# Attention with global tokens and a token/channel MLP: q, k and v of batch 1 loaded ahead of the first channel weights, and the order of two stages rewritten

## The chip, the cores and the metric

The kernel runs on one core of a Trainium2 chip. The metric is device time in microseconds (us). The core has five engines that run their own instruction lists in order and wait for each other by semaphores: TensorE (PE; its weight loads are listed as PEld), VectorE (DVE), ScalarE (ACT), GpSimd (POOL) and SyncE (SP, which here only issues DMAs). DMAs are issued by SP and by GpSimd and are carried out by 16 DMA engines.

## The reference

Eight batches of 576 tokens, eight heads of 64. Attention is banded (32 to either side) with eight global tokens that see all and are seen by all; its result x (576 x 512) goes through an MLP over the tokens (576 to 256 to 576) and one over the channels (512 to 1536 to 512), each added to its input.

```python
scores = scale * np.matmul(q, k.transpose(0, 1, 3, 2))
mask = (np.abs(pos[:, None] - pos[None, :]) <= 32) | is_global[:, None] | is_global[None, :]
attn = softmax(np.where(mask, scores, -1e9))
x = np.matmul(attn, v)                               # then heads side by side: 8 x 576 x 512
h = np.maximum(x.transpose(0, 2, 1) @ w_tok1, 0.0) @ w_tok2
u = x + h.transpose(0, 2, 1)
out = u + np.maximum(u @ w_ch1, 0.0) @ w_ch2
```

## The kernel before

The heads are taken in two groups of four (hg 0 and 1). Per batch the steps are:

- *Loads.* `load_qk(b)` issues on SP one DMA of k and five of q for each head group (float32); `load_v(b)` five DMAs of v in 256-byte rows, into one of two buffers. q and k in float32 have one buffer each. For batches 1 and 2, `load_qk` begins with a four-byte DMA (line 132) that reads a corner of the channel weights `wc1` or `wc2`: it waits until those have landed, and everything behind it on SP waits with it.
- *Casts and transposes.* `cast_k` (GpSimd, line 145), `cast_q` (ScalarE, line 141) and `vcast` (GpSimd, line 198) make 16-bit copies. `Xk` and `Xq` (VectorE, lines 217 and 225 to 229) transpose k and q of one head group.
- *Scores.* `S_step(b, hg, part)` makes banded scores in PSUM (line 255) and their exponentials on ScalarE (264 to 270); VectorE multiplies by the band (`S_mask`, 281), and GpSimd copies the global columns (`S_eg`, 284). `GK` makes the rows of the global queries (296, exponential 300, mask 303).
- *Output of attention.* `OG` (309, its result scaled into `rf` at 315) is the global rows' sum over v; `PV(b, tau)` (329 to 342) the product with v for each of five token tiles; its `norm` on VectorE (348, 349) divides and gives x.
- *Token MLP.* `M1` (362, relu on ScalarE 365), `M2` (378, sum into u on VectorE 383 and 386), `M3` (transposes of u on TensorE 396 and 406, copied to `uT` by VectorE 399 and 408). For batch 0 there are variants by tile, `M2t` (547, sum 550) and `M3t` (558, copy on ScalarE 559).
- *Channel MLP.* `M4(b, j)` for twelve j (416, relu on ScalarE 419) and `M5(b, tau, part)` (442, sum 446, store by SP 447). The last 64 tokens of two batches are done together, in the odd batch (`M4l`, 429, 433; 449, 451).

PSUM has three rings: `pss` (two buffers), `psv` (one) and `psm` (two, for M4, M5 and the fill matmuls).

The order is written out by hand. A prologue takes batch 0 through attention and token MLP, with fill matmuls on zeros (`fill`, line 102) between. Then comes one period per batch b: the twelve to fifteen M4 steps (list D4), then the M5 steps (list D5), into which `merge` mixes the attention and token MLP of later batches. `merge(sparse, dense)` walks two lists of (cost, function) and always takes the one whose middle lies earlier as a share of its list's total cost; `gap(c)` is an entry of cost c that does nothing. `weave(a, z)` spreads the entries of z evenly among those of a. `later` puts off masks and norms by some steps. In the prologue, SP issues v of batch 0, then (behind the wait for `wc1`) q, k and v of batch 1; GpSimd issues the token weights and all of `wc1` after three casts of v; the casts and transposes of batch 1 stand behind batch 0's token MLP; and `load_wc2` stands behind three casts of batch 1's v.

Of the kernel before, what the change touches and what calls it, by code (L numbers as in the profile page):

```python
# [17 lines left out]
P = 128  # L18
# [13 lines left out]
def kernel(  # L32
# [56 lines left out]
    def load_v(b):  # L89
        for c in range(NT):  # L90
            r0 = WIN if c == 0 else 0
            r1 = P - WIN if c == NT - 1 else P
            j0 = P * c - WIN + r0
            nc.sync.dma_start(
                out=n32v[b % 2][r0:r1, c], in_=v[b, :, j0 : j0 + (r1 - r0), :].rearrange("h p d -> p h d")
            )

    def fill(n):
        if n:
            ps = psm([P, 512], name="w")  # L100
            for _ in range(n):
                nc.tensor.matmul(ps, lhsT=zz[:, 0:P], rhs=zz, start=True, stop=True)  # L102
# [4 lines left out]
    def alloc_16(b):  # L107
        s = st[b]
        s["q16"] = stg.tile([P, 2, RK * D], F16, tag="q16", name=f"q16_{b}")
        s["k16"] = stg.tile([P, 2, RK * D], F16, tag="k16", name=f"k16_{b}")  # L110
# [16 lines left out]

    def load_qk(b):
        alloc_32(b)
        if b in (1, 2):  # L130
            src = wc1[0:1, 0, 512:514] if b == 1 else wc2[0:1, 4, 0:2]
            nc.sync.dma_start(out=st[b]["k32"].bitcast(F16)[0:1, 0, 0:2], in_=src)
        for hg in range(2):
            nc.sync.dma_start(
                out=st[b]["k32"][:, hg], in_=k[b, 4 * hg : 4 * hg + 4].rearrange("h (i r) d -> (h i) (r d)", i=32)
            )
            load_q(b, hg)

    def cast_q(b, hg, half):
        f = slice(half * 9 * D, half * 9 * D + 9 * D)  # L140
        nc.scalar.copy(out=st[b]["q16"][:, hg, f], in_=st[b]["q32"][:, hg, f])  # L141

    def cast_k(b, hg, half, eng=None):
        f = slice(half * 9 * D, half * 9 * D + 9 * D)
        (eng or nc.gpsimd).tensor_copy(out=st[b]["k16"][:, hg, f], in_=st[b]["k32"][:, hg, f])  # L145
# [84 lines left out]
            out=dst[:, 4, NG : NG + 64].rearrange("p (i r) -> p r i", r=2), in_=src[:, 16:18]  # L230
        )

    def load_wc1():
        for h0 in range(0, NJ, 4):
            nc.gpsimd.dma_start(
                out=wc1[:, :, P * h0 : P * h0 + 4 * P],
                in_=moe_w_ch1[:, P * h0 : P * h0 + 4 * P].rearrange("(c p) x -> p c x", p=P),
            )

    def load_wc2():  # L240
        for h0 in range(0, NJ, 4):
# [60 lines left out]
    def GK_mask(b):  # L302
        nc.vector.tensor_mul(out=lfs[b % 2][:, 0:LW], in0=lfs[b % 2][:, 0:LW], in1=mf)

    def OG(b, get):
        ps = get([P, 2, 512], name=f"og_{b}")
        for c in range(NT):
            for r in range(4):
                nc.tensor.matmul(  # L309
                    ps[32 * r : 32 * r + 32, 0, 0 : 2 * VW].rearrange("p (g x) -> p g x", g=2), lhsT=egs[b % 2][:, c, r],  # L310
                    rhs=vsh[b % 2][:, c, r::4, :], start=(c == 0), stop=(c == NT - 1),
                )
        rf = mb.tile([P, H, VW], F16, tag="rf", name=f"rf_{b}")
        for hg in range(2):
            nc.vector.tensor_tensor(  # L315
                out=rf[:, 4 * hg : 4 * hg + 4, :],
                in0=ps[:, 0, VW * hg : VW * hg + VW].unsqueeze(1).to_broadcast([P, 4, VW]),
                in1=dsel[:, 4 * hg : 4 * hg + 4].unsqueeze(2).to_broadcast([P, 4, VW]), op=ALU.mult,
            )
        st[b]["rf"] = rf  # L320
# [34 lines left out]
    def M1(b, get):  # L355
        s = st[b]
        x16 = x16s[b % 2]
        ps = get([P, 2, 512], name=f"a1p_{b}")
        for ch in range(NT):
            for tt in range(2):  # L360
                w = w1[:, ch, P * tt : P * tt + P] if ch < NT - 1 else w1l[:, b % 2, P * tt : P * tt + P]
                nc.tensor.matmul(ps[:, tt, :], lhsT=w, rhs=x16[:, ch, :], start=(ch == 0), stop=(ch == NT - 1))  # L362
        a1 = mb.tile([P, 2, DM], F16, tag="a1", bufs=1, name=f"a1_{b}")
        for tt in range(2):
            nc.scalar.activation(out=a1[:, tt], in_=ps[:, tt], func=AF.Relu)
        s["a1"] = a1
        s["u16"] = mb.tile([P, 4, DM], F16, tag="u16", name=f"u16_{b}")
        s["ul"] = st[b - 1]["ul"] if b % 2 else mb.tile([P, DM], F16, tag="ul", name=f"ul_{b}")
# [41 lines left out]
    def M4(b, j):  # L410
        s = st[b]
        if j == 0:
            s["b1"] = mb.tile([P, NJ, 512], F16, tag="b1", bufs=1, name=f"b1_{b}")
        ps = psm([P, 512], name=f"b1p_{b}_{j}")
        for cc in range(4):
            nc.tensor.matmul(  # L416
                ps, lhsT=wc1[:, cc, P * j : P * j + P], rhs=s["uT"][:, cc, :], start=(cc == 0), stop=(cc == 3)
            )
        nc.scalar.activation(out=s["b1"][:, j, :], in_=ps, func=AF.Relu)  # L419

    def M4l(b, jj):
        s = st[b]
# [36 lines left out]
    def run(fn):  # L459
        fn()  # L460
        for e in pending:
            e[0] -= 1
        for e in [e for e in pending if e[0] <= 0]:
            pending.remove(e)
            e[1]()
# [33 lines left out]
    def u_PV(b, tau, get):  # L499
        def f():  # L500
            norm = PV(b, tau, get)
            later(LAG_PV, norm)
        return f

    def phase_s(b):
        return [(0.5, u_S(b, hg, part)) for hg in range(2) for part in range(2)] + [(0.9, u_GK(b, psv))]

    def phase_og(b):
        return [(0.3, lambda: OG(b, psv))] + [(0.8, u_PV(b, t, psv if t % 2 else pss)) for t in range(NT)]

    def phase_m(b):
        u = [(0.9, lambda: M2(b, 0, psv)), (0.9, lambda: M2(b, 1, pss)), (0.5, lambda: M2(b, 2, pss))]
# [48 lines left out]
    def X_units(b):  # L561
        fs = [lambda: Xk(b, 0), lambda: Xq(b, 0), lambda: Xk(b, 1), lambda: Xq(b, 1)]
        return [(0.0, f) for f in fs]
# [106 lines left out]
    def eg_const(i):  # L670
        for g in range(2):
            nc.gpsimd.tensor_copy(out=egs[i][:, :, :, g, NG:16], in_=ohk.unsqueeze(2).to_broadcast([P, NT, 4, NG]))
# [4 lines left out]
    nc.gpsimd.dma_start(out=w1l[0:LAST, 0], in_=moe_w_tok1[S - LAST : S, :])  # L677
    vcast(0, (2,))
    nc.gpsimd.dma_start(out=w2[:, :, 0:S], in_=moe_w_tok2.rearrange("(c p) x -> p c x", p=P))
    load_wc1()  # L680
    fill(FILL[1])
    u_S(0, 0, 0)()
    fill(FILL[2])
# [10 lines left out]
    )  # L694
    nc.vector.tensor_scalar(out=mf[:, 4 * QS :], in0=it_f[:, 4 * P : S], scalar1=gpp, scalar2=hi8, op0=ALU.is_equal, op1=ALU.max)
    globals_k(0, nc.vector)
    nc.gpsimd.memset(n32v[1][0:WIN, 0], 0.0)
    nc.gpsimd.memset(n32v[1][P - WIN : P, NT - 1], 0.0)
    make_identity(nc, ident)
    nc.gpsimd.memset(x16s[0][LAST:P, NT - 1, :], 0.0)  # L700
    nc.gpsimd.memset(x16s[1][0:LAST, NT - 1, :], 0.0)
    eg_const(1)
    globals_(1, nc.gpsimd)
    globals_k(1)
    load_qk(1)
    load_v(1)
    u_S(0, 1, 1)()
    vcast(0, (3, 4), nc.scalar)
    fill(FILL[8])
# [1 line left out]
    fill(FILL[3])  # L711
    flush()
    GK_mask(0)
    for i, (_, f) in enumerate(phase_og(0)):
        run(f)
        fill(FILL[4] if i == 0 else FILL[5])
    flush()
    run(lambda: M1(0, pss))
    fill(FILL[6])
    for _, f in phase_m0():  # L720
        run(f)
# [6 lines left out]
    def gap(c):  # L728
        return [(c, lambda: None)]

    def G(b):
        return zero(lambda: globals_(b, nc.gpsimd), lambda: globals_k(b))
# [15 lines left out]
    def M1u(b):  # L748
        return [(2.2, lambda: M1(b, pss))]
# [7 lines left out]
                k += 1  # L757
        return o + z[k:]

    alloc_16(1)  # L760
    for hg in range(2):
        for half in range(2):
            cast_k(1, hg, half)
            cast_q(1, hg, half)
    nc.gpsimd.dma_start(out=w1l[LAST:P, 1], in_=moe_w_tok1[S - LAST : S, :])
    vcast(1, (0, 1, 2))
    load_wc2()
    vcast(1, (3, 4))
    load_qk(2)
    load_v(2)  # L770
    load_v(3)
    for _, f in X_units(1):
        f()

    for b in range(B):
        D4, D5 = dense(b)
        if b == 0:
            merge(gap(2.5) + phase_s(1), D4)
            merge(gap(2.0) + weave(phase_og(1) + M1u(1), C(2)) + weave(phase_m(1), G(2) + X_units(2)), D5)
            flush()  # L780
            gather(gq, q, 1)
            gather(gk, k, 1)
        elif b == 1:
            merge(VC(2) + phase_s(2) + gap(1.0) + weave(phase_og(2) + M1u(2), C(3)), D4)
            for _, f in G(3) + X_units(3):
                f()
            gather_t(gq, gqT, 1)
            gather_t(gk, gkT, 1)
            merge(VC(3) + weave(mix(phase_m(2), phase_s(3))[:-2], C(4)) + mix(phase_m(2), phase_s(3))[-2:], D5)
            flush()  # L790
        else:
            A, Bs = [], []
            if b + 1 < B:
                A += phase_og(b + 1) + M1u(b + 1)
                Bs += phase_m(b + 1)
            if b + 2 < B:
                A = G(b + 2) + weave(A, X_units(b + 2) + VC(b + 2))
                Bs = mix(Bs, phase_s(b + 2))
            if b + 3 < B:
                Bs = weave(Bs[:-2], C(b + 3)) + Bs[-2:]  # L800
            merge(A, D4)
            merge(Bs, D5)
            flush()
# [30 lines left out]
```

## Time and profile before

| | us |
|---|---|
| median of 3 runs (347.11 to 347.55) | 347.35 |
| the profiled execution | 348.57 |
| its span, first to last instruction | 346.8 |
| TensorE busy (92% of the span) | 319.5 |
| VectorE busy | 189.1 |
| ScalarE busy | 161.0 |
| GpSimd busy | 74.7 |
| mean granted TensorE clock, share of full | 0.973 |

The page gives each engine's busy time, and then rows of 40 digits: each digit is the busy share of a slice of 8.67 us in tenths, or the granted clock in tenths of full speed. A row of a timeline has the start, the length, the engine, the line of the kernel, the operation, out<-in, shapes and the count, and in brackets the idle time of that engine before it and what ended it. "PE b1p L416" is the matmul of line 416 that writes the tile b1p. A row of the waits view has who waited for whom, the total, how often, and the longest.

### The profile page before, as it was taken

What the parts mean: (1) busy time and instruction counts of PE and PEld (TensorE: products, weight loads), DVE (VectorE), ACT (ScalarE), POOL (GpSimd) and SP (SyncE); (2) the same over time, 40 slices, a digit from 0 to 9 for tenths busy, and PEclk for the clock granted to TensorE, in tenths of its full rate; (3) what the DMA queues carried; (4) which work ended last, traced back from release to release, by engine and by line L of the source; (5) the groups of instructions that cost most, each with busy time, mean ns of one, the idle gap of its engine ahead of it and who ended that gap; (6) DMA issues with size and microseconds to landing.
All of it is one profiled execution on the core that took longest, in us unless ns stands there. A gap on an engine that the chain in (4) does not pass through costs nothing.

```text
span 346.8 us, 7500 instructions
## 1 busy us (share of the span) xinstructions
PE 319.5 (92%) x3092; PEld 163.1 (47%) x3092; DVE 189.1 (55%) x355; ACT 161.0 (46%) x301; POOL 74.7 (22%) x154
## 2 busy tenths in 40 slices
PE   6599867998899999998899999999899999999994
PEld 2236323554356444544466445544456446444641
DVE  7695622648668468735680578546771484153021
ACT  5570448530866274428445373447453444503600
POOL 5791360154062014101420014002400000000000
PEclk9699969999899999999999999999999999999999
DMA  7998979999984969901892139101000111011012
GB/s 156 188 152 189 214 142 159 237 169 249 240 216 116 193 178 261 205 2 61 229 191 52 62 109 229 30 30 63 34 2 2 60 62 32 0 62 60 2 60 91
DMA packets 55706, 41.55 MB, mean 120 GB/s; under 512 B 40952, under 2 KB 46968, under 8 KB 55672
## 3 DMA queue, kind: packets, MB, share of 16 engines
q1 hardware_dynamic: 50104, 36.59, 44.2%
q0 software_dynamic: 5568, 4.49, 8.6%
q8 instruction: 24, 0.39, 0.5%
q14 instruction: 10, 0.08, 0.1%
HBM read 36.12 MB, written 9.44 MB: 131 GB/s over the span
## 4 chain that ended last, share of the span: by engine, by line
PE 70%; ACT 6%; DVE 5%; issue 2%; POOL 0%; POOLq 0%; DVEq 0%; ACTq 0%
PE op L442 23%; PE b1p L416 21%; PE hp L378 5%; PE a1p L362 4%; PE s L255 4%; DVE e_all L281 3%; PE b1lp L429 3%; PE pv L337 2%; PE pv L329 2%; ACT e_all L264 2%; PE pv L342 2%; PE pu L396 2%; ACT e_all L270 1%; ACT e_all L269 1%; PE og L309 1%
## 5 line engine op out<-in xcount | busy, mean ns | idle before, releaser
L416 PE MATMUL b1p<-uT,wc 128*128 128x512 f16 x384 | 95.1, 390 | 4.2 <-ACT b L419 4.2
L442 PE MATMUL op<-wc,b 128*128 128x512 f16 x384 | 94.6, 379 | 0.0
L419 ACT ACTIVATE b<-b1p 128x512 f16<-128x512 f32 x96 | 57.4, 601 | 66.6 <-PE b1p L416 66.3
L281 DVE TENSOR_TENSOR e_all<-e_all,bandm 128x1000 f16<-128x1000 f16 x64 | 39.5, 679 | 31.5 <-ACT e_all L270 31.4
L416 PEld LDWEIGHTS <-wc 128*128 128x128 f16 x384 | 34.8, 99 | 44.2 <-issue 11.0
L442 PEld LDWEIGHTS <-b 128*128 128x128 f16 x384 | 34.8, 98 | 38.7 <-issue 4.2
L264 ACT ACTIVATE e_all<-s 128x800 f16<-128x800 f32 x32 | 25.1, 838 | 41.2 <-PE s L255 40.9
L446 DVE TENSOR_TENSOR osb<-u,op 128x512 f32<-128x512 f16 x32 | 21.9, 686 | 34.1 <-PE op L442 30.2
L383 DVE TENSOR_TENSOR u<-x,hp 128x1024 f16<-128x1024 f16 x14 | 17.1, 1221 | 41.1 <-PE hp L378 41.0
L284 POOL COPY eg<-e_all 128x160 f16<-128x160 f16 x14 | 4.6, 328 | 155.8 <-DVE e_all L281 151.2
L255 PE MATMUL s<-qT,kT 32*128 32x200 f16 (+1 forms) x640 | 22.8, 249 | 9.4 <-DVE qT L203 4.3
L349 DVE TENSOR_TENSOR x<-pv,rr 128x512 f16<-128x512 f32 (+1 forms) x40 | 27.6, 691 | 1.4
L337 PE MATMUL pv<-vsh,e_all 128*128 128x66 f16 x320 | 27.6, 193 | 0.0
L145 POOL CAST k<-k 128x576 f16<-128x576 f32 x28 | 17.8, 666 | 44.6 <-DVE kT L217 25.0
L337 PEld LDWEIGHTS <-e_all 128*128 128x128 f16 x320 | 24.0, 97 | 5.0 <-issue 0.4
L255 PEld LDWEIGHTS <-kT 32*128 32x128 f16 x640 | 13.0, 97 | 25.9 <-issue 23.1
L198 POOL CAST vsh<-v 128x512 f16<-128x512 f32 x38 | 23.0, 640 | 4.7 <-DMA v<-in_v_dram 4.7
L141 ACT CAST q<-q 128x576 f16<-128x576 f32 x28 | 18.3, 682 | 11.4 <-DMA q<-in_q_dram 11.4
L342 PE MATMUL pv<-vsh,e_all 128*128 128x66 f16 x256 | 23.4, 193 | 0.0
L102 PE MATMUL w<-zz 128*128 128x512 f16 x66 | 21.1, 434 | 1.3 <-DVE p_i L154 1.3
L329 PE MATMUL pv<-rf,lf 128*128 128x264 f16 x80 | 21.7, 275 | 0.4 <-DVE rf L315 0.4
L217 DVE STREAM_TRANSPOSE kT<-k 128x576 int32<-128x576 int32 x16 | 19.9, 1245 | 0.8 <-DMA k<-in_k_dram 0.5
(133 smaller groups left out, 351.5 us busy)
## 6 DMA issues: line engine op xcount, KB each, us to landing
q<-in_q_dram SPq DMA_DIRECT2D x64, 128.0 KB
out_dram<-osb SPq DMA_DIRECT2D x32, 256.0 KB
k<-in_k_dram SPq DMA_DIRECT2D x14, 576.0 KB
v<-in_v_dram SPq DMA_DIRECT2D x24, 256.0 KB
v<-in_v_dram SPq DMA_DIRECT2D x16, 192.0 KB
wc<-in_moe_w_ch_dram POOLq DMA_DIRECT2D x6, 512.0 KB, 8.8
q<-in_q_dram SPq DMA_DIRECT2D x16, 64.0 KB
out_dram<-osb SPq DMA_DIRECT2D x8, 128.0 KB
```

The source lines that it names most:

```text
L198: (nc.scalar.copy if eng else nc.gpsimd.tensor_copy)(out=vsh[b % 2][:, c, :, 0:D], in_=n32v[b % 2][:, c])
L255: nc.tensor.matmul(tiles[r // 2][:, r % 2, off : off + n], lhsT=kT[rs, P * c : P * c + P, e], rhs=qf[rs, lo : lo + n, e], start=(e == 0), ...
L264: nc.scalar.activation(out=e2[:, :, 1:3, 64:EW], in_=ps[:, :, 0:400].rearrange("p h (c x) -> p h c x", c=2), func=AF.Exp, scale=scale)
L281: nc.vector.tensor_mul(out=eh, in0=eh, in1=bandm)
L329: nc.tensor.matmul(ps[:, hf, 0 : 4 * VW], lhsT=lfs[b % 2][:, QS * tau - sh : QS * tau - sh + P], rhs=s["rf"][:, 4 * hf : 4 * hf + 4, :], s ...
L337: nc.tensor.matmul(o, lhsT=e_all[:, h, tau, QS - sh : QS - sh + P], rhs=vs[:, tau, h, :], start=False, stop=last and tau == NT - 1,)
L342: nc.tensor.matmul(o, lhsT=e_all[:, h, tau + 1, 0:P], rhs=vs[:, tau + 1, h, :], start=False, stop=last)
L349: nc.vector.tensor_tensor(out=x16[r, tau, :].rearrange("p (f h x) -> p f h x", f=2, h=4), in0=pq[r, :, :, 0:D], in1=rr[r].unsqueeze(3).to_ ...
L416: nc.tensor.matmul(ps, lhsT=wc1[:, cc, P * j : P * j + P], rhs=s["uT"][:, cc, :], start=(cc == 0), stop=(cc == 3))
L419: nc.scalar.activation(out=s["b1"][:, j, :], in_=ps, func=AF.Relu)
L442: nc.tensor.matmul(ps, lhsT=w, rhs=wc2[:, j, :], start=(j == 0), stop=(j == NJ - 1))
L446: nc.vector.tensor_add(out=osb, in0=s["u16"][:, tau], in1=ps)
```

## The change

- `load_qk(1)` and `load_v(1)` move up on SP, right behind batch 0's v, and the wait of `load_qk(1)` for `wc1` goes.
- `load_wc1` is cut into its three DMAs. On GpSimd they move behind the identity, the memsets of x16 and the globals of batch 1; the second follows the k casts of head group 0, the third those of head group 1. The memsets of v's edges, `eg_const(1)` and the load of `w1l` follow them.
- The q casts of batch 1 (ScalarE) move to before `phase_og(0)` for head group 0 and to behind `M1(0)` for head group 1. The transposes of head group 0 move to behind `M1(0)`; those of head group 1 stay behind the token MLP, now after `load_qk(2)` and `load_v(2)`.
- In batch 0's M4, the relus of odd j go to VectorE.
- In period 0, the gap of 2.5 ahead of batch 1's scores goes; batch 2's casts, next loads and globals are all woven into batch 1's OG, PV and M1; of batch 2's transposes the first pair goes ahead of M2(1) and the second between the second M3(1) and the third. `load_v(3)` moves to the end of the period.
- OG takes a `pss` buffer in place of `psv`. From period 2 on, a gap of 1.7 stands ahead of `phase_og(b + 1)`.

```diff
     def load_qk(b):
         alloc_32(b)
-        if b in (1, 2):
-            src = wc1[0:1, 0, 512:514] if b == 1 else wc2[0:1, 4, 0:2]
-            nc.sync.dma_start(out=st[b]["k32"].bitcast(F16)[0:1, 0, 0:2], in_=src)
+        if b == 2:
+            nc.sync.dma_start(out=st[b]["k32"].bitcast(F16)[0:1, 0, 0:2], in_=wc2[0:1, 4, 0:2])
...
-    def load_wc1():
-        for h0 in range(0, NJ, 4):
-            nc.gpsimd.dma_start(
-                out=wc1[:, :, P * h0 : P * h0 + 4 * P],
-                in_=moe_w_ch1[:, P * h0 : P * h0 + 4 * P].rearrange("(c p) x -> p c x", p=P),
-            )
+    def load_wc1(i):
+        nc.gpsimd.dma_start(
+            out=wc1[:, :, 512 * i : 512 * i + 512],
+            in_=moe_w_ch1[:, 512 * i : 512 * i + 512].rearrange("(c p) x -> p c x", p=P),
+        )
...
-        nc.scalar.activation(out=s["b1"][:, j, :], in_=ps, func=AF.Relu)
+        if b == 0 and j % 2:
+            nc.vector.tensor_scalar_max(out=s["b1"][:, j, :], in0=ps, scalar1=0.0)
+        else:
+            nc.scalar.activation(out=s["b1"][:, j, :], in_=ps, func=AF.Relu)
...
-        return [(0.3, lambda: OG(b, psv))] + [(0.8, u_PV(b, t, psv if t % 2 else pss)) for t in range(NT)]
+        return [(0.3, lambda: OG(b, pss))] + [(0.8, u_PV(b, t, psv if t % 2 else pss)) for t in range(NT)]
...
     nc.gpsimd.dma_start(out=w2[:, :, 0:S], in_=moe_w_tok2.rearrange("(c p) x -> p c x", p=P))
-    load_wc1()
+    load_qk(1)
+    load_v(1)
...
     globals_k(0, nc.vector)
-    nc.gpsimd.memset(n32v[1][0:WIN, 0], 0.0)
-    nc.gpsimd.memset(n32v[1][P - WIN : P, NT - 1], 0.0)
     make_identity(nc, ident)
...
-    eg_const(1)
     globals_(1, nc.gpsimd)
     globals_k(1)
-    load_qk(1)
-    load_v(1)
+    alloc_16(1)
+    load_wc1(0)
+    cast_k(1, 0, 0)
+    cast_k(1, 0, 1)
+    load_wc1(1)
+    cast_k(1, 1, 0)
+    cast_k(1, 1, 1)
+    load_wc1(2)
+    nc.gpsimd.dma_start(out=w1l[LAST:P, 1], in_=moe_w_tok1[S - LAST : S, :])
+    nc.gpsimd.memset(n32v[1][0:WIN, 0], 0.0)
+    nc.gpsimd.memset(n32v[1][P - WIN : P, NT - 1], 0.0)
+    eg_const(1)
     u_S(0, 1, 1)()
...
     GK_mask(0)
+    for half in range(2):
+        cast_q(1, 0, half)
     for i, (_, f) in enumerate(phase_og(0)):
...
     run(lambda: M1(0, pss))
+    xs = X_units(1)
+    xs[0][1]()
+    xs[1][1]()
+    for half in range(2):
+        cast_q(1, 1, half)
     fill(FILL[6])
...
-    alloc_16(1)
-    for hg in range(2):
-        for half in range(2):
-            cast_k(1, hg, half)
-            cast_q(1, hg, half)
-    nc.gpsimd.dma_start(out=w1l[LAST:P, 1], in_=moe_w_tok1[S - LAST : S, :])
     vcast(1, (0, 1, 2))
     load_wc2()
     vcast(1, (3, 4))
     load_qk(2)
     load_v(2)
-    load_v(3)
-    for _, f in X_units(1):
-        f()
+    xs[2][1]()
+    xs[3][1]()
...
-            merge(gap(2.5) + phase_s(1), D4)
-            merge(gap(2.0) + weave(phase_og(1) + M1u(1), C(2)) + weave(phase_m(1), G(2) + X_units(2)), D5)
+            merge(phase_s(1), D4)
+            merge(gap(2.0) + weave(phase_og(1) + M1u(1), C(2) + G(2)) + X_units(2)[:2] + phase_m(1)[:5] + X_units(2)[2:] + phase_m(1)[5:], D5)
             flush()
             gather(gq, q, 1)
             gather(gk, k, 1)
+            load_v(3)
...
-                A += phase_og(b + 1) + M1u(b + 1)
+                A += gap(1.7) + phase_og(b + 1) + M1u(b + 1)
```

## The prediction

> **What bounds the kernel now.** I read the page first: the span, the forty slices, the chain that ended last.
>
> ```profile
> span 346.8 us, 7500 instructions
> PE   6599867998899999998899999999899999999994
> PEclk9699969999899999999999999999999999999999
> PE 70%; ACT 6%; DVE 5%; issue 2%; POOL 0%; POOLq 0%; DVEq 0%; ACTq 0%
> ```
>
> TensorE is the bound: nearly every slice from the sixth on is full, and its work makes up 70% of the chain. So a gain can only come from TensorE's idle time and from slices with a lowered clock: the fifth and sixth (about 43 us) and the tenth and eleventh (about 86 us). The view by windows measures both places (columns: busy us of TensorE, weight loads, VectorE, ScalarE, GpSimd, then granted clock, DMA share, GB/s).
>
> ```profile
> 40.20:46.40 6.20, 1.97 (x10) 0.86 (x9) 4.60 (x6) 3.03 (x6) 2.28 (x4) 0.89 1.07 171
> 46.40:52.00 5.60, 5.60 (x14) 1.92 (x14) 0.50 (x2) 1.92 (x4) 4.43 (x8) 0.51 0.69 127
> 52.00:64.20 12.20, 10.29 (x141) 4.42 (x139) 4.97 (x9) 11.10 (x24) 0.70 (x3) 1.00 0.93 183
> 83.60:86.10 2.50, 0.79 (x11) 0.32 (x10) 2.40 (x5) 0.00 (x0) 0.00 (x0) 0.98 1.18 311
> 86.10:89.40 3.30, 3.30 (x42) 1.47 (x41) 3.00 (x5) 2.11 (x3) 0.00 (x0) 0.50 1.04 269
> 89.40:98.60 9.20, 7.70 (x100) 3.06 (x92) 5.40 (x11) 8.43 (x21) 0.71 (x3) 1.00 0.96 238
> ```
>
> The first stretch is batch 0's first channel product (line 416), the fourth the start of batch 1's. Who is late in the first is in the timelines of TensorE, ScalarE and SP's queue:
>
> ```profile
> 40.19 1.89 PE L416 MATMUL b1p<-uT,wc 128*128 128x512 f16 x8
> 46.32 6.34 PE L416 MATMUL b1p<-uT,wc 128*128 128x512 f16 x16 [4.24 <-ACT b L419]
> 64.17 2.10 PE L442 MATMUL op<-wc,b 128*128 128x512 f16 x9
> ```
>
> ```profile
> 33.89 1.08 ACT L365 ACTIVATE a<-a1p 128x512 f16<-128x512 f32 x2 [8.92 <-PE a1p L362]
> 36.62 0.58 ACT L559 COPY uT<-pu 128x512 f16<-128x512 f16 x1 [1.65 <-PE pu L558]
> ...
> 44.41 1.36 ACT L141 CAST q<-q 128x576 f16<-128x576 f32 x2 [3.15 <-DMA q<-in_q_dram]
> 45.68 1.08 ACT L419 ACTIVATE b<-b1p 128x512 f16<-128x512 f32 x2
> ```
>
> ```profile
> 9.54 5.41 SPq L94 DMA_DIRECT2D v<-in_v_dram  x5
> 29.70 0.68 SPq L132 DMA_DIRECT2D k<-wc  x1
> 31.38 0.35 SPq L134 DMA_DIRECT2D k<-in_k_dram  x1
> ```
>
> The relu of line 419 stands behind two casts of batch 1's second q half, these behind a DMA, and that behind SP's wait for the channel weights until 29.70. TensorE idles 4.24 us, and then works 5.6 us at a clock of 0.51.
>
> **The change, part by part.** *A, batch 0's first channel product.* SP no longer waits for the weights, so the five-DMA v load of batch 0 (issued 9.54 to 14.95) is followed at once by q, k and v of batch 1: 31.38 - 14.95 = 16.4 us earlier. Nothing else on SP moves ahead of work of batch 0. On POOL the three weight loads move behind the identity, two memsets and the globals, and the second and third of them behind the k casts of one half each:
>
> ```profile
> 17.60 0.58 POOL L677 DMA_DIRECT2D w1l<-in_moe_w_tok_dram  x1
> 18.15 0.65 POOL L198 CAST vsh<-v 128x512 f16<-128x512 f32 x1
> 18.71 0.76 POOL L679 DMA_DIRECT2D w<-in_moe_w_tok_dram  x1
> 19.42 2.28 POOL L235 DMA_DIRECT2D wc<-in_moe_w_ch_dram  x3
> ...
> 26.87 0.33 POOL L211 COPY kg<-gkT 128x16 f16<-128x16 f16 x2
> 35.96 1.28 POOL L145 CAST k<-k 128x576 f16<-128x576 f32 x2 [8.77 <-DMA k<-in_k_dram]
> 41.91 1.28 POOL L145 CAST k<-k 128x576 f16<-128x576 f32 x2 [4.67 <-DMA k<-in_k_dram]
> 48.28 0.61 POOL L198 CAST vsh<-v 128x512 f16<-128x512 f32 x1 [0.69 <-DMA v<-in_v_dram]
> 48.83 2.26 POOL L242 DMA_DIRECT2D wc<-in_moe_w_ch_dram  x3
> ```
>
> Where four ScalarE casts and two transpose pairs now run decides the gain. The casts of the first q half come behind batch 0's last exponential and ahead of line 365; ScalarE idles 8.92 us there, so they cost nothing if q lands by 32. The second half's casts stand between line 365 and the copies of line 559: 34.97 to 36.33, in the 1.65 us hole, if q has landed by 35. Before, the last q half was there 44.41 - 31.38 = 13.0 us after the first issue. From 14.95, plus some 3 us in which batch 0's v is still arriving (its third cast is at 18.15), that is 31, the low bound. The high bound lets every GpSimd load issued meanwhile go first. The loads issued from 16.8 to 21.7 were so far landed at 29.70 that SP went on, some 13 us; without the third weight load that is about 10 us, and q comes at 41. I take the middle, 36, because the second weight load cannot start before the first k half has landed. Casts then end at 37.4 and the first copy is 0.8 us late: **a loss of 0.8**, between 0 and 5.7.
>
> The transposes of the first half fall into VectorE's hole between these two:
>
> ```profile
> 31.90 0.68 DVE L349 TENSOR_TENSOR x<-pv,rr 64x512 f16<-64x512 f32 x1
> 35.44 1.33 DVE L550 TENSOR_TENSOR u<-x,hp 128x512 f16<-128x512 f16 x2 [2.86 <-PE hp L547]
> 40.78 1.24 DVE L217 STREAM_TRANSPOSE kT<-k 128x576 int32<-128x576 int32 x1
> 41.88 1.01 DVE L225 STREAM_TRANSPOSE qT<-q 128x512 int32<-128x512 int32 x1
> 42.75 0.20 DVE L229 STREAM_TRANSPOSE qT<-q 128x64 int32<-128x64 int32 x1
> ```
>
> 2.4 us in 2.86: free. If the hole were gone they would cost 2.4.
>
> What TensorE then has to do until line 442 starts is the busy time of the first three windows less what the clock took: 1.97 + 5.60 + 10.29 - 5.6 x 0.49 = 15.1 us. The stage now lasts 64.17 - 40.19 = 24.0. The 1.9 us of idle in the third window are score products waiting for exponentials (ScalarE is busy 11.10 of 12.20). They shrink, since the score steps are spread from the stage's start and six of twelve relus leave ScalarE. A VectorE relu is not in the trace; the nearest row is a 0.69 us operation of the same shape out of PSUM, so six take 4.1 us on an engine that had 4.97 of 12.2 us of work. I take 0.6 us of idle (between 0 and 1.9). The stage becomes 15.7: **a gain of 8.3**.
>
> *B, batch 1's u and its transposes.* At 83.6 VectorE has batch 2's transposes between TensorE's needs:
>
> ```profile
> 78.13 0.69 DVE L446 TENSOR_TENSOR osb<-u,op 128x512 f32<-128x512 f16 x1 [3.37 <-issue]
> 82.48 1.26 DVE L217 STREAM_TRANSPOSE kT<-k 128x576 int32<-128x576 int32 x1
> 83.77 0.69 DVE L399 COPY uT<-pu 128x1024 f16<-128x1024 f16 x1
> 84.38 1.03 DVE L225 STREAM_TRANSPOSE qT<-q 128x512 int32<-128x512 int32 x1
> 85.38 0.65 DVE L399 COPY uT<-pu 128x1024 f16<-128x1024 f16 x1
> 86.09 0.85 PE L255 MATMUL s<-qT,kT 32*128 32x200 f16 x14 [0.36 <-DVE uT L399]
> ```
>
> The first pair moves ahead of the M2 sums, into the 3.37 us hole before 78.13, the second behind both uT copies. The copies then run at 82.5 and 83.2, and the scores start at about 84.0 in place of 86.09: 2.1 us. The half clock of 86.1 to 89.4 costs 3.3 x 0.5 = 1.65 more, but behind it ScalarE is busy 8.43 of 9.20 and would take most of it back. **A gain of 2.5**, between 2.1 and 3.7. The five DMAs of batch 3's v go behind batch 3's q and k and the first output stores on SP; their cast comes a whole period later, so I cost that at nothing.
>
> *C, OG later.* These waits can go:
>
> ```profile
> PE og L309 <- POOL eg L284: 2.4, 5, 0.9
> ```
>
> ```profile
> 134.98 0.27 PE L329 MATMUL pv<-rf,lf 128*128 128x264 f16 x1 [0.45 <-DVE rf L315]
> 170.30 0.47 PE L309 MATMUL og<-vsh,eg 128*32 128x132 f16 x20 [0.90 <-POOL eg L284]
> 98.69 0.47 PE L309 MATMUL og<-vsh,eg 128*32 128x132 f16 x20 [0.19 <-POOL eg L284]
> ```
>
> The one at 98.69 lies in a period without the new gap. With weight 1.7 of then 8.2, OG is written behind three M4 steps (2.6 us), more than the longest wait. 2.4 - 0.19 + 0.45 = 2.7, less 0.3 for a step that finds the output buffer not yet drained: **a gain of 2.4**, between -1 and 2.7.
>
> **Sum.** -0.8 + 8.3 + 2.5 + 2.4 = 12.4 us. The profiled run took 348.57 us (span 346.8), 1.2 above the median of 347.35; it becomes 336.2, and the median **335.0**.
>
> **Rivals.** *1. The second q half comes late.* GpSimd's casting loads share the 16 DMA engines with SP's queue; then the old stall stands again, ahead of line 559. Against it, both weight loads behind the first are held back by k casts; for it, the DMA share is already about 1 in these windows. At 41 the loss is 5.7 in place of 0.8, 340; with a half clock behind it 2.7 more, 342.7. The Trainium skill, "DMA: Bandwidth & Descriptors", Queues, rings and completion order, says that each engine changes between its queues packet by packet, which speaks for a shared rate and so for this rival; no run here shows the share yet. The skill's "TensorE: Matmul & The Clock Gate", HAM oscillation, warns of idle gaps above some 3.4 us; by it, a stall shorter than that would leave the clock alone. The trace disagrees: 0.50 from 86.1 on follows 1.71 us of idle in 2.5, and this measurement decides.
>
> *2. The second channel weights come late.* They are issued behind three casts of batch 1's v, today at 48.83, and SP passes its wait for their second part at 58.46:
>
> ```profile
> 58.46 0.65 SPq L132 DMA_DIRECT2D k<-wc  x1
> ```
>
> The first product with them now starts at 40.2 + 0.8 + 15.7 = 56.7. If they came no earlier than now (the third part at about 60), TensorE would wait some 3 us: 338. I expect the issue near 42, as v is sent 16.4 us earlier and shares the engines for 10.
>
> *3. OG later gives nothing*, since its sums and the x it feeds come late for M1: 337.4. Against it:
>
> ```profile
> 182.25 0.68 DVE L349 TENSOR_TENSOR x<-pv,rr 64x512 f16<-64x512 f32 x1
> ```
>
> M1 starts 2.5 us after this ends, and a fifth of that is what the closer spacing takes.
>
> *4. Slower.* SP's transfers get only what GpSimd's leave, so the second q half lands at 46, later than today's 44.41, though sent 16.4 us earlier. Casts end at 47.4, the copies of line 559 are 10.8 us late, and one half-clock stretch adds 2.7: a loss of 13.5 in place of 0.8, which turns the sum into a loss of 0.3: 347.7. Each further us of landing is a us slower, so 349.7 at 48. It decides from a landing at 45.7 on.
>
> *5. The loads do not move* (SP held by a buffer of batch 0): q's buffer is one, but batch 0's casts read it out before 14.95, so I see nothing that holds it. Then the old stall stays in another place: 347.
>
> **How the numbers follow.** Forecast 55% (own range 332 to 338), rival 1 18%, rival 2 10%, rival 3 10%, rival 4 5%, rival 5 2%. A range of 331.5 to 341.5 takes in the forecast with B and C at their ends, rivals 2 and 3 and most of rival 1. A measurement of this kernel can tell 0.2% (0.7 us) from no change. Faster: 0.93; the same 0.03 (rival 5 and the edge of 4); slower 0.04.
>
> **What would show it.** A right: batch 1's q casts on ScalarE end before 37.5, no wait of TensorE for line 419's result, a clock of 1.0 from 40 to 57, and line 442 starting at 56 to 58. Rival 1: the first copy of line 559 behind a q cast waiting for DMA. Rival 2: line 442 waiting for wc. B right: no transposes between the uT copies and no clock drop near the second M4 stage. C right: no TensorE wait for eg of line 284 after the first. The forecast fails if TensorE's busy time at full clock is not what I took, or if the stall returns in front of the copies.

## The result, and the profile after

The changed kernel takes 336.28 us (median; 335.81 to 337.78), the kernel before 347.23 in the same series: a ratio of 0.969, 95% interval 0.966 to 0.973. In a second series it took 337.15 against 347.17 (0.973, 0.970 to 0.976). The prediction was 335.0, within 331.5 to 341.5. The profiled execution took 337.78, with a span of 336.1.

The page of the changed kernel, the same rows as before:

```profile
span 336.1 us, 7493 instructions
PE   7499999988999999999999999999999999999994
PEclk9789999999999999999999999999999999999999
PE 78%; ACT 7%; DVE 6%; DMA 5%; issue 2%; POOL 1%; SPq 0%; ACTq 0%; DVEq 0%; POOLq 0%
```

Behind the first three slices the clock's row stays at 9, and no slice of TensorE's row is under 8 until the last. DMA is new in the chain, with 5%: the chain now runs through the load of batch 2's q, which makes TensorE wait (below).

Batch 0's first channel product is now line 414, its relus 420 (ScalarE) and 418 (VectorE), the second product 443. The timelines of TensorE, ScalarE and VectorE of the changed kernel around it:

```profile
41.18 1.03 PE L414 MATMUL b1p<-uT,wc 128*128 128x512 f16 x4
...
50.96 2.83 PE L414 MATMUL b1p<-uT,wc 128*128 128x512 f16 x12 [0.81 <-DVE b L418]
...
56.64 2.11 PE L443 MATMUL op<-wc,b 128*128 128x512 f16 x9
```

```profile
34.87 1.08 ACT L363 ACTIVATE a<-a1p 128x512 f16<-128x512 f32 x2 [6.24 <-PE a1p L360]
35.84 1.33 ACT L140 CAST q<-q 128x576 f16<-128x576 f32 x2
37.60 0.59 ACT L560 COPY uT<-pu 128x512 f16<-128x512 f16 x1 [0.42 <-PE pu L559]
```

```profile
33.49 1.24 DVE L216 STREAM_TRANSPOSE kT<-k 128x576 int32<-128x576 int32 x1
34.58 1.03 DVE L224 STREAM_TRANSPOSE qT<-q 128x512 int32<-128x512 int32 x1
35.46 0.21 DVE L228 STREAM_TRANSPOSE qT<-q 128x64 int32<-128x64 int32 x1
36.42 1.33 DVE L551 TENSOR_TENSOR u<-x,hp 128x512 f16<-128x512 f16 x2 [0.76 <-PE hp L548]
```

The stage lasts 56.64 - 41.18 = 15.5 us (before: 24.0). The second q casts need no wait for the DMA, and the first copy waits for TensorE, not for them. The first transposes lie where the 2.86 us hole was and leave 0.76 us of it. But the stage begins at 41.18, 1.0 later than before.

The end of batch 1's token MLP and the start of its M4, in the changed kernel's timelines of TensorE and ScalarE:

```profile
72.12 1.30 PE L376 MATMUL hp<-a,w 128*128 128x512 f16 x4 [1.56 <-ACT a L363]
78.36 0.66 PE L253 MATMUL s<-qT,kT 32*128 32x200 f16 x16
78.95 1.04 PE L414 MATMUL b1p<-uT,wc 128*128 128x512 f16 x4
```

```profile
70.10 1.48 ACT L140 CAST q<-q 128x576 f16<-128x576 f32 x2 [5.32 <-DMA q<-in_q_dram]
71.48 1.08 ACT L363 ACTIVATE a<-a1p 128x512 f16<-128x512 f32 x2
```

From the first score step on (78.36) the transposes are in nobody's way; ahead of it stands a wait that the kernel before did not have: M1(1)'s relu behind casts of batch 2 that wait for a DMA. In the later periods the waits for eg are gone, and two of 0.18 us for an output buffer are in their place:

```profile
PE og L307 <- POOL eg L282: 0.2, 1, 0.2
PE b1p L414 <- DVE osb L447: 0.4, 2, 0.2
PE b1p L414 <- ACT b L420: 0.7, 1, 0.7
```

The third row is one wait at the head of batch 2's M4. It was there in six of the nine runs below that have the gap ahead of OG, without a pattern that I could find; its cause stays open.

### The profile page after: what moved, and what is told of

Read it like the earlier page. It is cut to its first block, busy times and chain, and to the rows that moved or that the text cites. A ratio compares the mean times of both kernels' runs of the same rounds, so it can differ in the third digit from the quotient of the medians.

```text
span 336.1 us, 7493 instructions
## 1 busy us (share of the span) xinstructions
PE 316.1 (94%) x3092; PEld 162.2 (48%) x3092; DVE 193.9 (58%) x361; ACT 158.1 (47%) x295; POOL 75.5 (22%) x154
## 4 chain that ended last, share of the span: by engine, by line
PE 78%; ACT 7%; DVE 6%; DMA 5%; issue 2%; POOL 1%; SPq 0%; ACTq 0%; DVEq 0%; POOLq 0%
PE op L443 23%; PE b1p L414 22%; PE s L253 5%; PE hp L376 5%; PE a1p L360 4%; DMA q<-in_q_dram 4%; PE b1lp L430 3%; DVE e_all L279 3%; ACT e_all L262 3%; PE w L102 3%; PE pv L335 3%; PE pv L327 2%; PE pv L340 2%; PE gk L294 2%; PE pu L394 2%
## 5 line engine op out<-in xcount | busy, mean ns | idle before, releaser
L414 PE MATMUL b1p<-uT,wc 128*128 128x512 f16 x384 | 92.9, 379 | 1.9 <-DVE b L418 0.8
L420 ACT ACTIVATE b<-b1p 128x512 f16<-128x512 f32 x90 | 53.9, 599 | 62.6 <-PE b1p L414 62.3
L279 DVE TENSOR_TENSOR e_all<-e_all,bandm 128x1000 f16<-128x1000 f16 x64 | 42.0, 717 | 19.1 <-ACT e_all L268 19.0
L253 PE MATMUL s<-qT,kT 32*128 32x200 f16 (+1 forms) x640 | 22.0, 245 | 7.6 <-DVE qT L202 4.9
L144 POOL CAST k<-k 128x576 f16<-128x576 f32 x28 | 18.7, 698 | 39.5 <-DMA k<-in_k_dram 22.0
L197 POOL CAST vsh<-v 128x512 f16<-128x512 f32 x38 | 24.0, 667 | 11.6 <-DMA v<-in_v_dram 11.6
L102 PE MATMUL w<-zz 128*128 128x512 f16 x66 | 21.9, 448 | 1.3 <-DVE p_i L153 1.3
L376 PE MATMUL hp<-a,w 128*128 128x512 f16 x72 | 19.3, 378 | 2.7 <-ACT a L363 1.6
```

The costliest lines, as they stand in the source:

```text
L253: nc.tensor.matmul(tiles[r // 2][:, r % 2, off : off + n], lhsT=kT[rs, P * c : P * c + P, e], rhs=qf[rs, lo : lo + n, e], start=(e == 0), ...
L279: nc.vector.tensor_mul(out=eh, in0=eh, in1=bandm)
L376: nc.tensor.matmul(ps[:, i, :], lhsT=w2[:, ch, P * tau - sh : P * tau - sh + P], rhs=s["a1"][:, ch, :], start=(ch == 0), stop=(ch == 1),)
L414: nc.tensor.matmul(ps, lhsT=wc1[:, cc, P * j : P * j + P], rhs=s["uT"][:, cc, :], start=(cc == 0), stop=(cc == 3))
```

## The experiments

Theory: the change gains in three separate places, as predicted (A the first channel product, B the place of batch 2's transposes, C OG's start), and loses at two, one in the prologue and one at M2(1). The rivals are that the steps overlap, or that another part of the edit did it. The runs come in three series, each with the kernel before in it (medians 347.17, 347.56 and 347.16). The changed kernel itself ran in the first of them, with 337.15; from "The channel weights' three parts at once" on, the comparison with it goes across series.

### The changed kernel again, as the yardstick

> The changed kernel itself, as the yardstick for the three that run beside it. Expected 336.3 (335.8 to 337.8), 11 us below the kernel before. Its first score product started 0.55 us later in the profile of the change than in the profile of before (13.12 against 12.57), ahead of every edit. Theory: that is a difference between executions, so it moves by some tenths again here. Rival: the change itself makes it late, and it stands at 13.1 again.

Measured: 337.15. The first score product began at 12.54, so its 0.55 us in the first profile was a difference between executions. M1(0) still began at 32.38, 0.85 behind the 31.53 of before: this lateness belongs to the change.

### C undone: no gap ahead of OG

```diff
-                A += gap(1.7) + phase_og(b + 1) + M1u(b + 1)
+                A += phase_og(b + 1) + M1u(b + 1)
```

> The changed kernel without the gap of 1.7 ahead of OG; everything else stays. Theory (step C): the waits for eg come back, 0.9, 0.2, 0.9 and 0.2 us, and 0.4 for rf, while some 1.0 us of new waits at the head of M4 go: 1.6 slower than the changed kernel, 337.9. Rival (OG later gives nothing, the gain of the later periods came from something else, such as the output buffer of OG): within 0.4 of it.

Measured: 338.87, 1.7 slower than the changed kernel in the same series. The waits view of this kernel has the old row again, to the tenth:

```profile
PE og L307 <- POOL eg L282: 2.4, 5, 0.9
```

OG used the other PSUM ring here too, so that edit does not take these waits away; the gap does.

### All of batch 0's relus on ScalarE

```diff
-        if b == 0 and j % 2:
-            nc.vector.tensor_scalar_max(out=s["b1"][:, j, :], in0=ps, scalar1=0.0)
-        else:
-            nc.scalar.activation(out=s["b1"][:, j, :], in_=ps, func=AF.Relu)
+        nc.scalar.activation(out=s["b1"][:, j, :], in_=ps, func=AF.Relu)
```

> The changed kernel with all twelve relus of batch 0 on ScalarE. Theory (step A: the odd relus had to leave ScalarE, since it is the tight engine while scores and M4 run mixed): ScalarE gets six times 0.6 more in the 15.5 us of that stage, TensorE's idle time there grows from 1.0 to 2 to 3 us, so 1 to 2 slower, 337.3 to 338.3. Rival: the relu on VectorE is what makes TensorE wait (0.81 us at 50.96 for a relu behind the masks), ScalarE has room, and it is equal or up to 0.8 faster.

Measured: 336.26, 0.9 faster than the changed kernel beside it. The stage itself was 0.5 longer (41.37 to 57.24), and the later start met a shorter wait at M2(1) (0.32). So the theory's sign held for the stage, with a quarter to a half of its size, and not for the whole. Where the 0.9 comes from the traces do not show: the two profiled executions are 0.14 apart (336.64 and 336.78), and the changed kernel's own two series differ by as much as 0.9.

### Batch 2's second casts behind M1(1)

```diff
-            merge(gap(2.0) + weave(phase_og(1) + M1u(1), C(2) + G(2)) + X_units(2)[:2] + ...
+            merge(gap(2.0) + weave(phase_og(1), C(2)[:3]) + M1u(1) + C(2)[3:] + G(2) + X_units(2)[:2] + ...
```

> The changed kernel with the k and q casts of batch 2's second half (and the loads of batch 3 behind them) written behind M1(1), so that M1's relu does not stand behind casts that wait for a DMA. Theory: the 1.56 us wait of TensorE at 72.12 is ScalarE's order and goes, 1.3 to 1.6 faster, 334.8. Rival: it is the late DMA itself, which then holds up the second transposes of batch 2 and the later score steps instead: within 0.5 of the changed kernel.

Measured: 335.96, 1.2 faster than the changed kernel beside it. No wait at M2(1) is left, and no new one stands for it later. It was ScalarE's order: the q itself comes early enough for its own transposes. This wait also hides what happens ahead of it. In eight of the nine traces that keep the casts ahead of M1(1)'s relu, those of the changed kernel and of the edits below included, M2(1) begins 58.6 to 59.2 us behind the first score product, although M1(0) lies anywhere from 19.0 to 20.3 behind it; in the ninth (the last experiment) it is 59.9. With the casts behind the relu it is 57.1.

### The channel weights' three parts at once

```diff
     load_wc1(0)
+    load_wc1(1)
+    load_wc1(2)
     cast_k(1, 0, 0)
     cast_k(1, 0, 1)
-    load_wc1(1)
     cast_k(1, 1, 0)
     cast_k(1, 1, 1)
-    load_wc1(2)
```

> The changed kernel with all three parts of the first channel weights issued together, ahead of the k casts: the second part some 1 us and the third some 7 us earlier than in the change, and both inside the flight of batch 1's second q half. Theory (holding the parts back is what lets q land by 36): the second q half lands 2 to 4 us later, ScalarE's casts behind M1(0)'s relu wait for the DMA until 38 to 40, the copies of line 560 slip by 1.5 to 3.5, and the whole is 1.5 to 4 slower than the changed kernel (337.2 in its last series), 338.7 to 341. Rival: SP's queue keeps its rate beside GpSimd's loads, nothing slips, within 0.5.

Measured: 337.85 (ratio to before 0.972, 0.968 to 0.976), not told apart from the changed kernel's 337.15. ScalarE's timeline in it:

```profile
36.84 0.67 ACT L140 CAST q<-q 128x576 f16<-128x576 f32 x1
37.72 0.67 ACT L140 CAST q<-q 128x576 f16<-128x576 f32 x1 [0.21 <-DMA q<-in_q_dram]
38.60 0.59 ACT L560 COPY uT<-pu 128x512 f16<-128x512 f16 x1 [0.20 <-PE pu L559]
```

The cast waits 0.21 us and holds nothing up. But the place had become later too: the band masks took 4.36 us, M1(0) began 20.3 us behind the first score product (19.4 and 19.8 in the two profiles of the changed kernel), and the wait at M2(1) hid that. (One of the four masks took 1.13 us from 23.62 on, where it takes 0.67 undisturbed, though GpSimd's casts began only at 25.10; up to then it issued the three loads. What slowed that mask is open.) The second half of q landed at 37.72; in two kernels further down, which hold the parts back and whose cast waits for q as well, it landed at 36.90 and 36.26. That is 0.8 and 1.5 us earlier, of which half a us is SP's, which issued batch 1's k at 15.60 here (15.10 and 15.01). So holding the parts back does not bring the 5 us that lie between the prediction's 36 and its high bound; the reason it gives for taking the middle was too weak. The Trainium skill's "DMA: Bandwidth & Descriptors", Queues, rings and completion order (engines change between queues packet by packet), is not contradicted.

### B undone: batch 2's transposes in their old places

```diff
-            ... + X_units(2)[:2] + phase_m(1)[:5] + X_units(2)[2:] + phase_m(1)[5:], D5)
+            ... + phase_m(1)[:3] + X_units(2)[:1] + phase_m(1)[3:4] + X_units(2)[1:2] + phase_m(1)[4:5] + X_units(2)[2:3] + phase_m(1)[5:] + X_units(2)[3:], D5)
```

> The changed kernel with batch 2's transposes put back to where they stood before, between M2(1) and M3(1) and between the M3(1) steps. Theory (step B): the uT copies stand behind 2.4 us of transposes again, TensorE idles some 1.7 us before the second M4 stage and then meets a half clock for about 3.4 us: 2 to 3 slower than the changed kernel, 339.2 to 340.2. Rival: what bounds that stage is ScalarE's exponentials and the q casts, so the transposes' place is worth under 0.7.

Measured: 339.41 (0.978, 0.972 to 0.984), 2.3 above the changed kernel's 337.15 (1.9, if each is taken from the kernel before of its own series). TensorE's timeline has the three old waits again, 0.78, 0.57 and 0.35, and the next M4 starts 81.06 - 78.95 = 2.1 later than in the change. The window of the idle time:

```profile
79.02 0.38 PE L404 MATMUL pul<-ident,ul 128*128 128x128 f16 x4 [0.78 <-DVE uT L397]
79.98 0.26 PE L253 MATMUL s<-qT,kT 32*128 32x200 f16 x2 [0.57 <-DVE qT L228]
80.59 0.54 PE L253 MATMUL s<-qT,kT 32*128 32x200 f16 x14 [0.35 <-DVE uT L397]
81.06 1.04 PE L414 MATMUL b1p<-uT,wc 128*128 128x512 f16 x4
```

```profile
77.00:82.00 5.00, 3.29 (x38) 1.63 (x35) 4.97 (x7) 0.84 (x2) 0.00 (x0) 1.00 1.02 267
82.00:87.00 5.00, 3.64 (x51) 1.60 (x51) 4.00 (x8) 4.73 (x11) 0.00 (x0) 1.00 0.92 248
```

The same 1.7 us of idle, and yet a clock of 1.00: the half clock that followed in the kernel before is not a sure consequence of it.

### The kernel before, its stall filled with matmuls

The edit computes nothing new: 19 matmuls on zeros into a buffer that nobody reads.

```diff
+        if b == 0 and j == 2:
+            pf = pss([P, 2, 512], name="pf")
+            for _ in range(19):
+                nc.tensor.matmul(pf[:, 0], lhsT=zz[:, 0:P], rhs=zz, start=True, stop=True)
```

> The kernel before, with 19 matmuls on zeros (4.1 us of TensorE work into a spare buffer) written just ahead of batch 0's third M4 step, where TensorE idles 4.24 us. The stall itself stays. Theory (step A: the half clock from 46 to 52 is made by the idle time, and cost 2.7): the clock stays at 1.0 there and the stage is 2.0 to 2.7 shorter: 344.5 to 345.2. Rival: the clock falls all the same, or the exponentials behind it take the gain back: 346.5 to 347.2.

Measured: 346.06 against 347.56 (0.996, 0.994 to 0.998): 1.5 faster. TensorE's timeline and the window that had a clock of 0.51:

```profile
42.46 4.26 PE L417 MATMUL pf<-zz 128*128 128x512 f16 x19
46.56 3.62 PE L420 MATMUL b1p<-uT,wc 128*128 128x512 f16 x16
...
61.69 2.10 PE L446 MATMUL op<-wc,b 128*128 128x512 f16 x9
```

```profile
46.40:52.00 5.60, 5.44 (x40) 2.29 (x39) 0.51 (x2) 3.94 (x7) 4.40 (x8) 1.00 0.73 118
```

Batch 1's q comes no earlier, and the matmuls behind the stall begin at 46.56 (before: 46.32), but the clock stays at 1.00, and the sixteen matmuls that took 6.34 take 3.62. The stage is 61.69 - 40.73 = 21.0 us, 3.0 shorter. So the idle time made the half clock there. The timed gain is half of the stage's. The profiled execution of the kernel before, from which the 24.0 comes, is one of its longest, with a mean clock as low as any (348.57 us, 0.973); the 13 executions in this series have a median clock of 0.979, the filled kernel's ten one of 0.985. By an estimate from these two, the clock gave back 0.006 x 347 = 2.1 us, nearer to the timed 1.5 than to 3.0. So the usual execution seems to lose less to the half clock than the profiled one did; that is not shown.

### GpSimd's first k casts later

```diff
     load_wc1(0)
+    nc.gpsimd.memset(n32v[1][0:WIN, 0], 0.0)
+    nc.gpsimd.memset(n32v[1][P - WIN : P, NT - 1], 0.0)
+    eg_const(1)
     cast_k(1, 0, 0)
...
-    nc.gpsimd.memset(n32v[1][0:WIN, 0], 0.0)
-    nc.gpsimd.memset(n32v[1][P - WIN : P, NT - 1], 0.0)
-    eg_const(1)
     u_S(0, 1, 1)()
```

> The changed kernel with GpSimd's k casts of the first half moved behind the memsets of v's edges and eg_const(1), so they start some 1.7 us later and mostly behind VectorE's band masks of batch 0's second half. In the change these four masks took 3.60 us in place of 2.44 while GpSimd cast, and TensorE reached M1(0) 0.85 to 0.97 us later than before. Theory (the casts slow the masks): the masks take 2.4 to 2.9, OG and M1(0) start 0.4 to 0.9 earlier, 336.3 to 336.8 against 337.2. Rival: the delay has another cause and M1(0) stays at 32.3 to 32.5.

Measured: 337.60 (0.972, 0.968 to 0.976), no faster. But the mechanism is as the theory has it. The band masks of batch 0's second half, in the kernel before and in the changed kernel; in the latter GpSimd's casts lie beside them, and both are slow:

```profile
22.26 2.44 DVE L281 TENSOR_TENSOR e_all<-e_all,bandm 128x1000 f16<-128x1000 f16 x4
```

```profile
22.80 3.60 DVE L279 TENSOR_TENSOR e_all<-e_all,bandm 128x1000 f16<-128x1000 f16 x4 [0.15 <-ACT e_all L268]
```

```profile
23.16 2.12 POOL L144 CAST k<-k 128x576 f16<-128x576 f32 x2
30.28 1.28 POOL L144 CAST k<-k 128x576 f16<-128x576 f32 x2 [4.31 <-DMA k<-in_k_dram]
```

With the casts later, VectorE's masks are quick again:

```profile
22.65 2.57 DVE L279 TENSOR_TENSOR e_all<-e_all,bandm 128x1000 f16<-128x1000 f16 x4
```

From the first score product to M1(0) are 19.0 us (32.07 - 13.11), as in the kernel before (31.53 - 12.57); in the changed kernel 19.4 and 19.8. What it won was given back: q of batch 2 did not come earlier with it, and M2(1) began 58.8 us behind the first score product, where the changed kernel has 59.0 and 58.6. Its wait in this trace (the changed kernel's two have 1.56 and 0.8):

```profile
PE hp L376 <- ACT a L363: 1.7, 1, 1.7
```

With M1(0) back in its place, batch 1's second q half shows when it lands. ScalarE's timeline in this kernel, and behind it the same row of the next one:

```profile
36.90 0.67 ACT L140 CAST q<-q 128x576 f16<-128x576 f32 x1 [0.83 <-DMA q<-in_q_dram]
```

```profile
36.26 0.67 ACT L140 CAST q<-q 128x576 f16<-128x576 f32 x1 [0.73 <-DMA q<-in_q_dram]
```

The first copy of line 560 is 0.3 and 0.2 us late behind it, and the first channel product still begins 8.66 us behind M1(0), as in the kernel before.

### Both reorderings together

The two edits of "Batch 2's second casts behind M1(1)" and "GpSimd's first k casts later".

> The changed kernel with both reorderings that were tried singly: the k casts behind the memsets and eg_const(1), and batch 2's second casts behind M1(1). Singly the first brought M1(0) back by 0.9 us, and the whole gained nothing, since the wait for ScalarE's casts at M2(1) grew to 1.73 us; the second took 1.2 off. Theory (the gain of the first was given back at that wait): together they are worth 1.2 + 0.9 = 2.1, so 335.1 where the changed kernel has 337.2. Rival: what the first gains is lost elsewhere too: 336.0, as the second alone.

Measured: 335.07 against 347.16 (0.967, 0.963 to 0.971), 2.1 below the changed kernel's 337.15. M1(0) begins at 31.53 and M2(1) waits for nothing:

```profile
66.00 1.89 PE L360 MATMUL a1p<-x,w 128*128 128x512 f16 x8
67.72 0.59 PE L360 MATMUL a1p<-x,w1l 128*128 128x512 f16 x2
68.15 1.46 PE L443 MATMUL op<-wc,b 128*128 128x512 f16 x6
69.45 1.03 PE L376 MATMUL hp<-a,w 128*128 128x512 f16 x4
```

That the first alone gained nothing, the second 1.2 and both 2.1 is what a gain given back at the second place would look like, and this is the lowest median of all. It is not shown, though. The changed kernel's two series differ by 0.9, and the intervals of the three ratios overlap. The traces are nearer to the rival: against the second edit alone, M1(0) lies 0.6 earlier behind the first score product, but M2(1) and the next M4 only 0.2 (56.9 for 57.1, 63.5 for 63.7), and the profiled executions took 334.82 and 335.00. What is shown is the wait at M2(1) and its end.

### Both, and all relus on ScalarE

The edits of the last one and of "All of batch 0's relus on ScalarE".

> The same two reorderings, and all relus of batch 0 on ScalarE, which alone took 0.9 off the changed kernel (part of it a shorter wait at M2(1), which the reordering already takes). Theory: another 0.4 to 0.8 off, 334.3 to 334.7. Rival: with the wait at M2(1) gone the relus on VectorE are worth their place in the first stage (that stage was 0.5 us longer without them): 335.1 to 335.6.

Measured: 335.72 (335.09 to 336.88), 0.65 above the last one beside it (334.63 to 337.14). The numbers are the rival's, but the two overlap, and the profiled executions are 0.27 apart. With the wait at M2(1) gone, the stage is 15.9 long (40.12 to 55.98) against 15.5, and the next M4 begins 0.2 later behind the first score product. So the relus on VectorE are worth some tenths at most; in the changed kernel's own order the stage's 0.5 was waited away at M2(1).

### A alone

The changed kernel with B and C undone, by the edits shown above; OG's PSUM ring and the moved loads and globals of period 0 stay.

> The changed kernel with the old places of batch 2's transposes and without the gap ahead of OG: only step A (and the store and load order around it) is left. Theory (the steps add up): 337.2 + 1.7 + 2.1 = 341.0, which puts A at some 6.3 below the kernel before. Rival (the steps overlap, so that one takes what the other leaves): 339.5 or less.

Measured: 341.09 (0.983, 0.979 to 0.988). The steps add up, 337.15 + 1.7 + 2.3 = 341.1, and do not overlap.

### Batch 2's q and k sent earlier

```diff
-            nc.sync.dma_start(out=st[b]["k32"].bitcast(F16)[0:1, 0, 0:2], in_=wc2[0:1, 4, 0:2])
+            nc.sync.dma_start(out=st[b]["k32"].bitcast(F16)[0:1, 0, 0:2], in_=wc2[0:1, 0, 0:2])
```

> The changed kernel with SP's wait ahead of batch 2's k and q tied to the first third of the second channel weights instead of the second: q of batch 2 leaves some 3 us earlier. Theory (the wait of 0.8 to 1.7 us at M2(1) is the q load's lateness): it goes, 0.8 to 1.5 faster than the changed kernel, 335.7 to 336.4, like moving the casts. Rival: the earlier q slows the last two thirds of the weights, and TensorE waits for them in the first M5 instead, equal or slower.

Measured: 335.91 (0.967, 0.963 to 0.971), which fits the theory, but the profile does not. SP's timeline in it:

```profile
50.63 0.68 SPq L131 DMA_DIRECT2D k<-wc  x1
55.20 0.35 SPq L133 DMA_DIRECT2D k<-in_k_dram  x1
```

The four-byte DMA is issued 3 us earlier (in the changed kernel 53.61), but k only 0.8 us earlier (there 55.99), since SP waits 3.8 us for those four bytes to land. ScalarE's second casts began at 70.70, no earlier than the 70.10 of the changed kernel, and TensorE waited 2.25 us. In this execution (338.79 us) the clock fell behind that wait:

```profile
70.00:72.50 2.50, 0.25 (x3) 0.01 (x1) 0.69 (x1) 1.80 (x4) 2.04 (x4) 0.98 0.90 179
72.50:76.00 3.50, 3.50 (x9) 1.21 (x9) 1.22 (x1) 0.43 (x1) 2.89 (x5) 0.52 1.10 264
```

Inconclusive: the profiled execution is not like the timed ones (335.01 to 336.62 but for it), and the times alone do not tell this edit from the changed kernel's own spread.

## Why the prediction was right

**A, the stage: right.** Forecast 15.7 us, measured 15.5, no wait for q, a clock of 1.00. Its idle time was 1.0 us and not 0.6, most of it a relu on VectorE behind the band masks (0.81), and its busy time 14.5 and not 15.1. The filled kernel shows that the idle time made the half clock, which I had only read off the granted clock; how much of it the usual execution had stays open.

**A, the loss ahead of it: about the right number, by luck.** Forecast 0.8 us from a late second q half. The landing was forecast well, at 36, where the two kernels that show it have 36.90 and 36.26, but it held up the first copy by no more than 0.3 us there and the stage not at all. The stage was late by 1.0 and 0.85 (in the two profiles) because GpSimd's k casts slowed VectorE's masks (3.60 and 3.84 us in place of 2.44). I had checked every engine's order at that place, and not whether two engines slow each other. Rival 1 thus had its late transfer in the wrong place: it did come, one batch later.

**B: 2.3 (or 1.9) measured for 2.5 forecast,** 2.1 in the trace, the idle time as worked out. The 0.4 that the forecast added for the clock was not seen: with B undone the clock stayed at 1.00. And the same stage lost 0.8 to 1.6 us at M2(1), which no step of the forecast had. I had moved batch 2's casts one place up with the rest, and had checked when batch 2's q was needed by its own transposes, but not what stood behind its casts on ScalarE: M1(1)'s relu. In the kernel before, the casts stood ahead of that relu too, but their wait of 4.62 us ended as TensorE began M1(1), so it cost nothing:

```profile
74.48 1.24 ACT L141 CAST q<-q 128x576 f16<-128x576 f32 x2 [4.62 <-DMA q<-in_q_dram]
76.83 1.08 ACT L365 ACTIVATE a<-a1p 128x512 f16<-128x512 f32 x2 [1.11 <-PE a1p L362]
```

With M1(1) 7.5 us earlier, and SP's k for batch 2 issued only 4.4 us earlier (55.99 for 60.41), it did cost. This is the same fault that A removed, one batch on.

**C: 1.7 for 2.4.** The waits for eg went, and undoing the gap brings them back. What took their place is larger than my 0.3: 0.4 for the output buffer, and perhaps the 0.7 at batch 2's M4, which I cannot explain.

**The sum.** 8.5 - 0.9 + 2.1 - 1.2 + 1.7 = 10.2, where the medians give 10.0 and 11.0; forecast 12.4. The total came out near the forecast although it left out a loss of 1.2, because the range was wide enough for that and for C's 0.7; that part is luck, and the three gains are not. Rivals 2 to 5 did not come: line 443 never waits for the weights, OG's gap pays, and SP issues batch 1's k at 15.12, held by no buffer.

## What to carry to other kernels

When a stage moves up, go through each in-order engine once more at its new time: a wait that ended just before it mattered is the next stall, and the fault just removed is the likeliest one to be met there. Put an instruction that waits for a transfer behind everything that does not need it, on its engine. And a gain or a loss ahead of a wait for a transfer does not show in the time while that wait stands (M2(1) kept its place while M1(0) moved by 1.4 us), so look at where a stage begins as well as at the total before a reordering is dropped or kept.

## What was not expected of the hardware

VectorE's masks (two 16-bit inputs from SBUF) and GpSimd's casts from 32 to 16 bits slow each other: four masks 3.60 us (3.84 in the second profile) in place of 2.44, two casts 2.12 in place of 1.28. The Trainium skill's "GPSIMD Engine Reference", Key points, says that GpSimd shares its SBUF interfaces with VectorE and contends with instructions that have two SBUF inputs; the traces agree, and give the price as 1.2 to 1.4 us on 2.4.

The clock fell to half for 3.5 us behind a wait of 2.25 us, and in the kernel before behind 1.71 us of idle in 2.5; in the kernel with B undone the same 1.7 us left it at 1.00. So neither the length of the gap alone nor the 3.4 us of the Trainium skill's "TensorE: Matmul & The Clock Gate", HAM oscillation, tells whether it falls.
